# The first batch's stage rebuilt: weight words split in PSUM, V through DRAM, two taps in one GpSimd instruction, and new order tables

## The chip, the cores and the metric

The kernel runs on one core of one Trainium2 chip. The time is the device time of one execution in microseconds (us). Engines go by the profile's names: PE (TensorE matmuls), PEld (its weight loads), DVE (VectorE), ACT (ScalarE), POOL (GpSimd), SP (the engine that issues all of this kernel's DMAs).

## What is computed

A causal convolution over seven positions, with softmax weights per position and head, is followed by a low-rank mixing along the sequence and a two-layer network:

```python
w = softmax(weight_gen, axis=-1)                       # (8, 4224, 8 heads, 7 taps)
out[b, s, h, g] = sum_k w[b, s, h, k] * x_pad[b, s + k, h, g]    # 24 columns to a head
u = out + (out^T @ U @ V)^T                            # U: 4224 x 32, V: 32 x 4224
y = u + max(u @ w_ch1, 0) @ w_ch2                      # 192 -> 768 -> 192
```

Shapes are 8 batches of 4224 rows of 192 columns. `x` and `weight_gen` are float32. The four weights `U`, `V`, `w_ch1`, `w_ch2` come as float64, and the kernel reads them as pairs of 32-bit words.

## The kernel before

**Blocks and chunks.** Partition p holds the 33 rows p*33 to p*33+32 of a batch. Three of them on all partitions (384 rows) are a block `i`, 11 to a batch, 88 in all. The convolution of the same rows is chunk `c`. For a chunk each of the seven taps is one multiplication of 128x576 elements (`conv_mul`, tile `p`), and the products are added into the PSUM tile `acc`; the result is `y_c`.

**The stage of the first batch.** Before block 0 can start, all eleven chunks of batch 0 must be done, because the mixing needs their sum over the whole sequence (`z_first`, then `z_sum`, `z_split`, `z_copy`, which gives `zcat`). Chunk 11 of batch 1 is laid there too. In the same stage the weights are taken apart. A float64 is turned into a rounded fp32r part, and a remainder of what that leaves, by `f64_split`: in step 0 and 1 ACT converts the high and the low word, in 2 and 3 DVE shifts and sets the sign, in 4 ACT writes the rounded part, in 5 to 7 or 8 DVE makes the scale, the low word's value, the difference and the sum. There are twelve such sets (three of U, three of V, three of w1, three of w2); six have five DVE instructions and six have six, 66 in all. Their tiles (`..._t`, `..._s`, `..._lf`, `..._r`, `..._hi`, with the set's name ahead, `w_` for w2) lie in SBUF. V's parts are then put into `vcat` by 48 ACT copies of 32 partitions each (`v_copies`).

Taps of this stage are multiplied by POOL (weights from SBUF, tile `wr`) or by DVE (weights from a copy in PSUM, tile `wq`). The products are added by PE (a product with the identity `ident`, `conv_pe`), by DVE (`conv_add`), and the first one of a chunk by an ACT copy. The last addition of each chunk, which writes `y`, is DVE's.

**What sets the order.** Each engine carries out its instructions in the order in which the program lists them, and so does SP with its DMAs. The list is made by numbers: `at(time, work)` collects the pieces of work, and `issue()` emits them sorted by `time`. The tables `F_...` do so for the first stage, `GHI` to `ZM` for the blocks after it. A block has six time units. Its PE work is `mm1` (five matmuls for each of six tiles `h`, from `hi` and `lo`, the two parts of the transposed `u`) and `mm2` (into `ab`, from `gh` and `gl`); ACT makes `hi` and `gh`, DVE makes `lo`, `gl` and the output `o`, and ACT's `ab` seed fills `ab` before `mm2`. POOL goes on with the convolution about a batch ahead. The first block of a batch, and block 1 (`is_late`), take the transposed `u` from PSUM and not by way of DRAM.

```python
def u_lo(i, part):
    ...
    nc.vector.tensor_tensor(like(i, lo), u_from(i, part), like(i, hi[:n].bitcast(F32)), op=ALU.subtract)
```

The line number of nearly all instructions in the profile is 30, the helper that pins their order, so they are told apart by their tiles.

Of the kernel before, what the change touches and what calls it, by code (L numbers as in the profile page):

```python
# [44 lines left out]
def conv_moe_kernel(  # L45
# [23 lines left out]
    P = 128  # L69
# [35 lines left out]
    def fetch(n):  # L105

        if n >= len(PIECES):
# [77 lines left out]
    def f64_split(name, raw, n, hi, shaped, lo=None, rest=None, after=None):  # L185


        tiles = {}

        def tmp(what, dt=F32):  # L190
            if what not in tiles:
                tiles[what] = first.tile(
                    [P, CH], dt, tag=what, name=f"{name}_{what}",
                    bufs=3 if what in ("r", "hi", "lf") else 2,
                )[:, :n]
            return tiles[what]
# [12 lines left out]
        def ti():  # L209
            return tmp("t").bitcast(I32)  # L210
# [4 lines left out]
                tmp("t"), high.bitcast(F32), AF.Copy, scale=2.0**-112  # L215
            ),
            lambda: nc.scalar.copy(tmp("lf"), low.bitcast(U32)),
# [6 lines left out]
            lambda: nc.scalar.copy(top(), shaped(tmp("t"))),  # L224
# [4 lines left out]
                low_word(), shaped(tmp("lf")), 2.0**-52,  # L229
# [3 lines left out]
        if rest is not None:  # L233
            steps.append(
                lambda: nc.vector.tensor_tensor(
                    rem(), shaped(tmp("t")), top().bitcast(F32), op=ALU.subtract
                )
            )
        else:
            steps += [  # L240
                lambda: nc.vector.tensor_tensor(
                    shaped(tmp("r")), shaped(tmp("t")), top().bitcast(F32),
                    op=ALU.subtract,
                ),
                lambda: nc.vector.tensor_tensor(
                    rem(), shaped(tmp("r")), low_word(), op=ALU.add
                ),
            ]
# [69 lines left out]
    def prep_v():  # L318
# [3 lines left out]
        for p0 in range(0, PQ, step):  # L322
# [3 lines left out]
            for q in range(Q):  # L326
# [7 lines left out]
                after=lambda *parts: v_copies(p0, m, *parts),  # L334
            )

    def v_copies(p0, m, top, rem, low_word):
        def one(q, i):
            src = (top, rem, low_word, top)[i]().bitcast(F32)
            ps = q * R + p0  # L340
# [5 lines left out]
        return [lambda q=q, i=i: one(q, i) for q in range(P // R) for i in range(4)]  # L346
# [13 lines left out]
    def softmax(n_):  # L360
# [15 lines left out]
        nc.vector.tensor_scalar(sm, sm, 1e-9, None, op0=ALU.add)  # L376
# [27 lines left out]
    wqs = {}  # L404

    def conv_wq(c):
        n, jl = where[c]
        wq = ps_first.tile([P, 512], F32, tag="wq", name=f"wq_{c}", bufs=2)
        wqs[c] = wq[:, : T * H * K].rearrange("p (t h k) -> p t h k", t=T, h=H)
        nc.scalar.copy(wqs[c], ws[n][:, jl : jl + T])  # L410

    def conv_mul(c, k, mixed=False):
        n, jl = where[c]
        j = c % NB * T
        pool = pf if c < NB and k in (0, 2, 4) else pp
        pk = pool.tile([P, T, D], F32, tag="p", name=f"p_{c}_{k}")
        eng, w = (nc.vector, wqs[c]) if mixed else (nc.gpsimd, ws[n][:, jl : jl + T])
# [6 lines left out]
        prods[(c, k)] = pk  # L424

    def conv_done(c):
# [6 lines left out]
    def conv_first(c, pool):  # L433


        acc = pool.tile([P, 1024], F32, tag="acc", name=f"acc_{c}")
        accs[c] = halves(acc)
        if c > 1:
            nc.scalar.copy(accs[c], split3(prods.pop((c, 0))))
        else:  # L440
            conv_pe(c, 0)

    def conv_pe(c, k):

        pk = split3(prods.pop((c, k)))
        for i in range(2):
            nc.tensor.matmul(
                accs[c][:, i], ident, pk[:, i],
                start=(k == 0), stop=True, skip_group_check=True,
            )  # L450

# [172 lines left out]
    def d_tile(i, part, pool=None):  # L624
        d = (pool or ps_d).tile(
            [P, 512], F32, tag="wq" if pool else "d", name=f"d_{i}_{part}",
            bufs=2 if pool else 1,
# [193 lines left out]
    GHI = [0.683, 0.44, 0.78, 0.441, 0.818, 0.797]  # L821
    GLO = [1.427, 1.631, 1.807, 1.418, 1.153, 1.282]
    AB = [-0.507, -0.72, -0.687]
    OH = [2.136, 2.535, 1.934]
    OA = [2.941, 3.066, 2.841]
    UC = 5.253
    UT = -6.896
    UB = -5.473
    UH = [-1.541, -0.531]
    UL = [-1.009, -0.309]  # L830
    DS = [-2.383, -0.797]
    US = [-11.643, -8.974]
    UM = [-9.93, -8.655]
    UTK = [-9.566, -8.514]
    MUL = [-1.341, 0.905, -0.084, 1.787, 2.403, 2.46, 4.888]
    ADD = [1.149, 2.181, 3.355, 3.892, 4.643, 6.066]
    LA = 0.434
    SHORT = [15, 16, 17, 18, 19]
    SOFT = [-10.851, -8.336, -5.978, -4.698, -4.059, -2.592]
    DN = 1.833  # L840
    YH = 1.075
    YHL = 2.399
    YL = 4.355
    ZS = 5.19
    ZP = 6.235
    ZC = 6.666
    M1 = [-0.161, 0.323, -0.511, 0.043, -0.273, 0.135]
    M2 = [0.641, 0.346, 0.26, 0.394, -0.086, 0.837]
    DM = [-2.201, -0.724]
    ZM = 4.559  # L850
# [15 lines left out]
    F_FIRST = [6.54, 14.42, 17.88, 23.56, 30.37, 35.91, 37.83, 43.54, 50.85, 58.04, 61.28, 71.62]
# [144 lines left out]
```

## Time and profile before

| What | us |
|---|---|
| Median of 3 runs (lowest, highest) | 1141.16 (1139.52, 1141.96) |
| The profiled execution's own time | 1141.85 |
| Its span, from first to last instruction | 1139.8 |
| Busy in the span: PE, PEld | 1085.3, 1048.1 |
| Busy in the span: DVE, POOL, ACT | 995.1, 902.9, 831.7 |

The span is 2.05 us shorter than the time of the same execution. The share of busy time is an average over two unlike stages: PE is busy for 0.5 to 0.8 of the time in the first five of the page's 40 slices, and for 0.9 or more from then on, but for the last one. A row of a view by lines reads: engine, operation, tile written from tiles read, partitions x elements, count, then the busy time of the group, the mean of one in ns, and the idle time of the engine just before them.

### The profile page before, as it was taken

How to read it: one execution, taken by the hardware profiler on the slowest of the kernel's cores; microseconds unless marked ns; L12 is line 12 of the kernel's file. 1: busy time of each engine (PE TensorE's matmuls, PEld its weight loads, DVE VectorE, ACT ScalarE, POOL GpSimd, SP SyncE). 2: the span in 40 equal slices, each digit the busy share in tenths (PEclk: the TensorE clock that was granted, in tenths of full speed). 3: DMA queues.
4: the chain of work that ended last, by engine and by line, in shares of the span. 5: the costliest groups of instructions: out<-in, count | busy, mean ns of one | idle time of the engine just before them, and what ended most of it. 6: DMA issues, size and time to landing. Idle time of an engine off the chain costs nothing.

```text
span 1139.8 us, 20500 instructions
## 1 busy us (share of the span) xinstructions
PE 1085.3 (95%) x6619; PEld 1048.1 (92%) x6619; DVE 995.1 (87%) x1750; ACT 831.7 (73%) x1967; POOL 902.9 (79%) x719
## 2 busy tenths in 40 slices
PE   5786699999999999999999999999999999999998
PEld 3665599999999999999999999999999999999998
DVE  7998899999999999989999999999999989855553
ACT  5567477768777877778777877777777877776674
POOL 6784899999999999999999899999999899500000
PEclk8888799999999999999999999999999999999999
DMA  6223143434343443344334434344334332222321
GB/s 212 93 80 102 32 113 105 127 99 135 104 130 103 113 125 110 112 117 134 107 114 115 126 112 120 98 124 124 115 106 127 95 93 73 85 73 83 95 74 52
DMA packets 123308, 121.33 MB, mean 106 GB/s; under 512 B 78857, under 2 KB 97609, under 8 KB 123074
## 3 DMA queue, kind: packets, MB, share of 16 engines
q1 hardware_dynamic: 123202, 120.04, 36.4%
q8 instruction: 52, 0.85, 0.3%
q14 instruction: 54, 0.44, 0.1%
HBM read 68.38 MB, written 51.61 MB: 105 GB/s over the span
## 4 chain that ended last, share of the span: by engine, by line
PE 75%; DVE 13%; ACT 4%; issue 4%; POOL 2%; DMA 1%; SPq 0%; DVEq 0%; ACTq 0%; POOLq 0%
PE h L30 36%; PE ab L30 34%; PE zp L30 3%; DVE acc L30 2%; DVE lo L30 2%; ACT vcat L30 2%; PE u L30 2%; POOL p L30 2%; DVE sq L30 1%; DVE gl L30 1%; ACT gh L30 1%; DVE sm L30 1%; DVE p L30 1%; DVE o L30 1%; DVE y L30 1%
## 5 line engine op out<-in xcount | busy, mean ns | idle before, releaser
L30 POOL TENSOR_TENSOR p<-x,wr 128x576 f32<-128x576 f32 x585 | 735.7, 1289 | 44.5 <-DVE acc L30 26.9
L30 PE MATMUL ab<-w2c,gh 128*128 128x384 f32 x1584 | 511.6, 353 | 0.0
L30 ACT ACTIVATE gh<-h 128x384 fp32r<-128x384 f32 x528 | 260.4, 493 | 154.8 <-PE h L30 152.3
L30 PE MATMUL ab<-w2c,gl 128*128 128x192 f32 x1584 | 365.4, 256 | 0.0
L30 DVE SCALAR_TENSOR_TENSOR gl<-h,gh 128x384 fp32r<-128x384 f32 x528 | 286.8, 543 | 84.3 <-ACT gh L30 79.7
L30 DVE TENSOR_TENSOR acc<-acc,p 128x576 f32<-128x576 f32 x390 | 293.8, 753 | 18.2 <-ACT acc L30 14.1
L30 PEld LDWEIGHTS ab<-w2c,gh 128*128 128x128 f32 x1584 | 298.6, 189 | 0.2 <-ACT gh L30 0.2
L30 PEld LDWEIGHTS ab<-w2c,gl 128*128 128x128 f32 x1584 | 296.9, 189 | 0.0
L30 PE MATMUL h<-lo,w1s 128*128 128x384 f32 x528 | 181.9, 345 | 3.7 <-DVE lo L30 2.6
L30 PE MATMUL h<-hi,w1h 128*128 128x384 f32 x528 | 181.0, 343 | 1.0 <-DVE gl L30 0.9
L30 PE MATMUL h<-hi,w1s 128*128 128x384 f32 x528 | 179.9, 341 | 0.0
L30 PE MATMUL h<-hi,w1l 128*128 128x384 f32 x528 | 179.9, 341 | 0.0
L30 PE MATMUL h<-lo,w1h 128*128 128x384 f32 x528 | 179.4, 340 | 0.0
L30 ACT ACTIVATE ab<-u 128x384 f32<-128x384 f32 x264 | 130.4, 494 | 6.6 <-DVE o L30 6.0
L30 DVE TENSOR_TENSOR lo<-uT,hi 128x384 fp32r<-128x384 f32 (+1 forms) x158 | 126.8, 802 | 1.0 <-ACT hi L30 0.3
L30 ACT COPY o<-ab 128x192 f32<-128x192 f32 x264 | 85.2, 323 | 55.0 <-PE ab L30 55.0
L30 ACT CAST hi<-uT 64x384 fp32r<-64x384 f32 (+1 forms) x237 | 121.6, 513 | 1.9
L30 POOL TENSOR_TENSOR yhl<-y,yhl 128x576 fp32r<-128x576 f32 x77 | 111.0, 1441 | 11.3 <-ACT yhl L30 11.1
L30 PEld LDWEIGHTS h<-lo,w1s 128*128 128x128 f32 x528 | 99.5, 188 | 14.0 <-DVE lo L30 13.4
L30 PEld LDWEIGHTS h<-hi,w1h 128*128 128x128 f32 x528 | 100.9, 191 | 3.9 <-DVE gl L30 3.6
L30 DVE TENSOR_TENSOR o<-ab,o 128x192 f32<-128x192 f32 x264 | 91.5, 346 | 12.5 <-ACT o L30 7.7
L30 PEld LDWEIGHTS h<-hi,w1s 128*128 128x128 f32 x528 | 99.5, 188 | 0.4 <-ACT hi L30 0.4
(107 smaller groups left out, 1288.8 us busy)
## 6 DMA issues: line engine op xcount, KB each, us to landing
out_dram<-o SPq DMA_DIRECT2D x88, 288.0 KB, 2.8
turn<-sq SPq DMA_DIRECT2D x348, 72.0 KB, 1.9
x<-in_x_dram SPq DMA_DIRECT2D x77, 288.0 KB, 3.6
uT<-turn SPq DMA_DIRECT2D x87, 192.0 KB, 2.4
uT<-turn SPq DMA_DIRECT2D x87, 96.0 KB, 2.5
wr<-in_weight_gen_dram SPq DMA_DIRECT2D x15, 336.0 KB, 4.1
x<-in_x_dram SPq DMA_DIRECT2D x7, 504.0 KB, 5.5
wr<-in_weight_gen_dram SPq DMA_DIRECT2D x9, 252.0 KB, 3.9
```

The costliest lines, as they stand in the source:

```text
L30: return self.tc.keep_in_program_order(call(*args, **kwargs))
```

## The change

Five things are changed.

1. `f64_split` keeps the words in PSUM: `t` in the bank of pool `ps_d`, the low word and the first difference in one bank `px` (tiles `pt_..._t` and `pt_..._x`). The low word's product, the scale `s` and the rounded part stay in SBUF.
2. V's parts are stored to DRAM (nine stores), read back into a tile `vq` of all 128 partitions (sixteen loads, one `vq` buffer), and put into `vcat` by four ACT copies.
3. POOL multiplies two taps in one instruction of 128x1152 elements (`conv_mul2`): of the 84 taps of the stage 46 go in 23 such pairs and 8 alone on POOL, 30 on DVE (before: 53 alone on POOL, 31 on DVE). The weights for DVE's taps now share one PSUM bank of three slots.
4. The additions: before, PE has 52 of them and DVE 22, eleven of which wrote `y` in batch 0 and one in chunk 11. After, PE has 59, DVE 16, and ACT copies eleven finished sums to `y`. The +1e-9 of the softmax goes from DVE to ACT, in the whole kernel.
5. The first stage's order is a written list, `FIRST`, instead of times, and 29 of the 30 tables for the blocks have new numbers.

```diff
@@ f64_split
+        def bank(what):
+            if what not in tiles:
+                pool, tag = (ps_d, "d") if what == "t" else (ps_first, "px")
+                tiles[what] = pool.tile([P, 512], F32, tag=tag, name=f"pt_{name}_{what}")[:, :n]
+            return tiles[what]
...
         def ti():
-            return tmp("t").bitcast(I32)
+            return bank("t").bitcast(I32)
...
-            lambda: nc.scalar.copy(tmp("lf"), low.bitcast(U32)),
+            lambda: nc.scalar.copy(bank("x"), low.bitcast(U32)),
...
-                    shaped(tmp("r")), shaped(tmp("t")), top().bitcast(F32),
+                    shaped(bank("x")), shaped(bank("t")), top().bitcast(F32),
                     op=ALU.subtract,
@@ V
-            nc.scalar.copy(
-                vcat[i * R : (i + 1) * R, :, ps : ps + m],
-                src[q * R : (q + 1) * R].rearrange("r (p j) -> r j p", j=NJ),
-            )
+            nc.sync.dma_start(
+                vts[i][:, p0 * NJ : p0 * NJ + n], parts[i]().bitcast(F32)
+            )
...
+    def v_load(q):
+        PQ = P // (P // R)
+        vqs[q] = first.tile([P, PQ * NJ], F32, tag="vq", name=f"vq_{q}", bufs=1)
+        for i, k in enumerate((0, 1, 2, 0)):
+            nc.sync.dma_start(
+                vqs[q][i * R : (i + 1) * R], vts[k][q * R : (q + 1) * R]
+            )
+
+    def v_place(q):
+        PQ = P // (P // R)
+        nc.scalar.copy(
+            vcat[:, :, q * PQ : (q + 1) * PQ],
+            vqs.pop(q).rearrange("r (p j) -> r j p", j=NJ),
+        )
@@ softmax
-        nc.vector.tensor_scalar(sm, sm, 1e-9, None, op0=ALU.add)
+        nc.scalar.activation(sm, sm, AF.Copy, bias=1e-9)
+        yield
@@ convolution
+    def conv_mul2(c, k):
+
+        n, jl = where[c]
+        j = c % NB * T
+        pk = pf.tile([P, 2, T, D], F32, tag="p2", name=f"p_{c}_{k}{k + 1}")
+        x0 = xt[:, j + k : j + k + T, :]
+        w0 = ws[n][:, jl : jl + T, :, k]
+        nc.gpsimd.tensor_tensor(
+            pk.rearrange("p k t (h g) -> p k (t h) g", h=H),
+            bass.AP(
+                tensor=x0.tensor, offset=x0.offset,
+                ap=[x0.ap[0], [D, 2], [G, T * H], [1, G]],
+            ),
+            bass.AP(
+                tensor=w0.tensor, offset=w0.offset,
+                ap=[w0.ap[0], [1, 2], [K, T * H], [0, G]],
+            ),
+            op=ALU.mult,
+        )
...
+    def conv_copy(c):
+        y = yp.tile([P, T, D], F32, tag="y", name=f"y_{c}")
+        nc.scalar.copy(split3(y), accs.pop(c))
+        ys[c] = y
@@ tables of the blocks (two of 29)
-    UH = [-1.541, -0.531]
+    UH = [-1.831, -0.529]
-    AB = [-0.507, -0.72, -0.687]
+    AB = [-0.793, -0.666, -0.577]
...
@@ the first stage's order
+    FIRST = """
+        R W1 S0 x0 S0 S0 U0 S1 S0 S1 S0 S0 S1 S0 Q0 S1 U1 M0.0v S1 M0.1d S1 P0.0 F0.0t x1
...
+        d1 C9.3 Y11.6
```

In `FIRST` a letter names the work and the numbers what it is for: P is a step of a split set, M a multiplication (by v DVE, p POOL, d POOL for two taps), F and A additions, Y a finished chunk.

How the change moves instructions is read off the two programs, at three places. Names are as in the profile with their numbers: `w22` and `w24` are two sets of w2, `p_11_6` is tap 6 of chunk 11, `p_11_45` the pair of its taps 4 and 5.

DVE at the end of the first stage, before:

```order
L30 TENSOR_SCALAR w22_s_795<-w22_t_682 128x384
L30 TENSOR_TENSOR w24_r_797<-w24_t_752,w2c_108 128x384
L30 SCALAR_TENSOR_TENSOR w22_lf_693<-w22_lf_693,w22_s_795 128x384
L30 TENSOR_TENSOR w22_r_807<-w22_t_682,w2c_108 128x384
L30 SCALAR_TENSOR_TENSOR w24_lf_755<-w24_lf_755,w24_s_793 128x384
L30 TENSOR_TENSOR w2c_108<-w22_r_807,w22_lf_693 128x2x192
L30 TENSOR_TENSOR w2c_108<-w24_r_797,w24_lf_755 128x2x192
L30 TENSOR_TENSOR zcat_0_826<-zr_0_820,zcat_0_826 32x192
L30 TENSOR_TENSOR acc_11_818<-acc_11_818,p_11_3_813 128x2x288
L30 TENSOR_TENSOR acc_11_818<-acc_11_818,p_11_1_824 128x2x288
L30 TENSOR_TENSOR p_11_6_838<-x_90,wq_11_801 128x576
L30 TENSOR_TENSOR lo1_0_109<-d_0_1_809,hi1_0_835 64x384
```

The same place after:

```order
L30 TENSOR_TENSOR acc_11_732<-acc_11_732,p_11_12_721 128x2x288
L30 TENSOR_SCALAR w24_s_756<-pt_w24_t_728 128x384
L30 TENSOR_TENSOR acc_11_732<-acc_11_732,p_11_12_721 128x2x288
L30 SCALAR_TENSOR_TENSOR w24_lf_765<-pt_w24_x_739,w24_s_756 128x384
L30 TENSOR_TENSOR pt_w24_x_739<-pt_w24_t_728,w2c_108 128x384
L30 TENSOR_TENSOR acc_11_732<-acc_11_732,p_11_45_749 128x2x288 x2
L30 TENSOR_TENSOR w2c_108<-pt_w24_x_739,w24_lf_765 128x2x192
L30 TENSOR_TENSOR y_11_789<-acc_11_732,p_11_6_767 128x576
L30 TENSOR_TENSOR zcat_0_795<-zr_0_793,zcat_0_795 32x192
L30 TENSOR_TENSOR lo0_0_801<-d_0_0_780,hi0_0_799 128x384
L30 TENSOR_TENSOR lo1_0_109<-d_0_1_784,hi1_0_804 64x384
```

Where two sets of w2 stood back to back, with all operands in SBUF, one set now stands between the additions of chunk 11, each of its instructions with an operand in PSUM; chunk 11 ends ahead of `zcat` and not after `lo`.

POOL at the start of the first stage, before:

```order
L30 TENSOR_TENSOR wr_0_92<-wr_0_92,mx_0_137 128x168
L30 TENSOR_TENSOR wr_0_92<-wr_0_92,sm_0_138 128x168
L30 TENSOR_TENSOR p_0_2_146<-x_90,wr_0_92 128x576
L30 TENSOR_TENSOR p_0_5_156<-x_90,wr_0_92 128x576
L30 TENSOR_TENSOR wr_1_130<-wr_1_130,mx_1_163 128x504
L30 TENSOR_TENSOR p_0_3_179<-x_90,wr_0_92 128x576
L30 TENSOR_TENSOR p_0_1_186<-x_90,wr_0_92 128x576
```

The same place after:

```order
L30 TENSOR_TENSOR wr_0_92<-wr_0_92,mx_0_126 128x168
L30 TENSOR_TENSOR wr_1_124<-wr_1_124,mx_1_136 128x504
L30 TENSOR_TENSOR wr_0_92<-wr_0_92,sm_0_127 128x168
L30 TENSOR_TENSOR p_0_12_159<-x_90,wr_0_92 128x1152
L30 TENSOR_TENSOR wr_1_124<-wr_1_124,sm_1_137 128x504
L30 TENSOR_TENSOR p_0_56_183<-x_90,wr_0_92 128x1152
```

The softmax of the second piece of weights (`wr_1`) moves ahead of the first taps, and the taps go in pairs.

ACT in a block after the first stage (blocks 35 and 36), before:

```order
L30 ACTIVATE gh_35_4_7050<-h_35_4_7030 128x384
L30 CAST hi1_36_7072<-uT1_36_6936 64x384 x2
L30 ACTIVATE ab_35_0_7075<-u_35_6642 128x384
L30 ACTIVATE gh_35_5_7081<-h_35_5_7063 128x384
L30 COPY o_34_6938<-ab_34_2_7014 128x192
```

The same place after:

```order
L30 ACTIVATE gh_35_4_7004<-h_35_4_6985 128x384
L30 ACTIVATE ab_35_0_7010<-u_35_6598 128x384
L30 CAST hi1_36_7020<-uT1_36_6869 64x384 x2
L30 ACTIVATE gh_35_5_7030<-h_35_5_7012 128x384
L30 COPY o_34_6891<-ab_34_2_6976 128x192
```

The seed of `ab` now stands ahead of the two copies that make `hi1` for the next block. PE's own order in the blocks is the same but for `zr`, one matmul in a batch (fp32, as two passes), which stands one `mm1` tile later.

More of the change, by code (lines that the diff above doesn't have):

```diff
@@ L333, in prep_v, with v_stores, one @@
                 f"v{p0}", raw, n, None, flat, rest=True,
-                after=lambda *parts: v_copies(p0, m, *parts),
+                after=lambda *parts: v_stores(p0, n, *parts),
             )
[L337 to L340, printed above, removed]
-            nc.scalar.copy(
-                vcat[i * R : (i + 1) * R, :, ps : ps + m],
-                src[q * R : (q + 1) * R].rearrange("r (p j) -> r j p", j=NJ),
-            )
-        return [lambda q=q, i=i: one(q, i) for q in range(P // R) for i in range(4)]
+    vts = []
+    def v_stores(p0, n, *parts):
+        while len(vts) < NU:
+            vts.append(
+                dram.tile(
+                    [P, P // (P // R) * NJ], F32, tag=f"vt{len(vts)}",
+                    name=f"vt{len(vts)}", bufs=1,
+                )
+            )
+        def one(i):
+            nc.sync.dma_start(
+                vts[i][:, p0 * NJ : p0 * NJ + n], parts[i]().bitcast(F32)
+            )
+        return [lambda i=i: one(i) for i in range(NU)]
+    vqs = {}
+    def v_load(q):
[11 more added lines that the diff above has]
+        )
     works = {}
@@ L424, in conv_mul @@
         prods[(c, k)] = pk
+    def conv_mul2(c, k):
[15 more added lines that the diff above has]
+            op=ALU.mult,
+        )
+        for i in range(2):
+            prods[(c, k + i)] = pk[:, i]
     def conv_done(c):
@@ L448, in conv_pe, with conv_vector, conv_last @@
                 accs[c][:, i], ident, pk[:, i],
-                start=(k == 0), stop=True, skip_group_check=True,
+                start=begin, stop=True, skip_group_check=True,
             )
+    def conv_vector(c, k):
+        acc = accs[c]
+        nc.vector.tensor_tensor(acc, acc, split3(prods.pop((c, k))), op=ALU.add)
+    def conv_copy(c):
+        y = yp.tile([P, T, D], F32, tag="y", name=f"y_{c}")
+        nc.scalar.copy(split3(y), accs.pop(c))
+        ys[c] = y
+    def conv_last(c, k):
+        y = yp.tile([P, T, D], F32, tag="y", name=f"y_{c}")
+        nc.vector.tensor_tensor(
+            split3(y), accs.pop(c), split3(prods.pop((c, k))), op=ALU.add
+        )
+        ys[c] = y
     accs = {}
@@ new lines, in conv_moe_kernel @@
+    DS = [-2.436, -0.869]
+    US = [-11.65, -8.874]
+    UM = [-9.793, -8.798]
+    UTK = [-9.258, -8.463]
+    MUL = [-1.341, 1.206, -0.084, 1.462, 2.534, 2.46, 4.808]
+    ADD = [1.149, 2.101, 3.355, 3.866, 4.615, 6.279]
+    LA = 0.659
+    SHORT = [15, 16, 17, 18, 19]
+    SOFT = [-9.854, -7.411, -5.03, -4.293, -6.756, -3.712, -3.227]
+    DN = 1.925
+    YH = 1.011
+    YHL = 0.839
+    YL = 2.929
+    ZS = 5.206
+    ZP = 6.344
+    ZC = 6.726
+    M1 = [0.517, 0.011, -0.164, 0.107, -0.273, 0.378]
@@ L887, in conv_moe_kernel @@
-        for n in range(5):
-            for time in F_SOFT[n]:
-                at(time, soften, n)
-        for c in range(NB + 1):
-            at(F_WQ[c], conv_wq, c)
-            for k in range(K):
-                at(F_MUL[c][k], conv_mul, c, k, F_BY[c][0][k] == "v")
-            at(F_DONE[c], conv_done, c)
-            at(F_FIRST[c], conv_first, c, ps_a if c % 2 else ps_first)
-            for k in range(1, K):
-                at(F_ADD[c][k - 1], conv_pe if F_BY[c][1][k - 1] == "t" else conv_add, c, k)
-            if c < NB:
-                at(F_Z[c], z_first, c)
@@ L900, in conv_moe_kernel @@
-        at(F_TURN[0], u_turn, 1)
-        at(F_TURN[1], u_back, 1)
-        for time, work in zip(F_END, (
-            (z_sum, 0), (z_split, 0), (z_copy, 0), (d_turn, 0, 0), (d_mix, 0, 0),
-            (u_hi, 0, 0), (u_lo, 0, 0), (d_turn, 0, 1), (d_mix, 0, 1), (u_hi, 0, 1),
-            (u_lo, 0, 1),
-        )):
-            at(time, *work)
-        issue()
+        segs = ((0, 9), (9, 18), (18, 30), (30, 39))
+        for code in FIRST.split():
+            kind, by = code[0], code[-1]
+            n = [int(i) for i in code[1:].rstrip("pdvta").split(".") if i]
+            if kind == "U":
+                prep_load(n[0], kinds[F_KIND[n[0]]])
+            elif kind == "P":
+                prep_step(*n)
+            elif kind == "C":
+                copy_one(*n)
+            elif kind == "W":
+                fetch(*n)
+            elif kind == "x":
+                x_load(0, *segs[n[0]])
+            elif kind == "S":
+                soften(*n)
+            elif kind == "Q":
+                conv_wq(*n)
+            elif kind == "M":
+                conv_mul2(*n) if by == "d" else conv_mul(*n, by == "v")
+            elif kind == "D":
+                conv_done(*n)
+            elif kind == "F":
+                conv_first(*n, by)
+            elif kind == "A":
+                conv_pe(*n) if by == "t" else conv_vector(*n)
+            elif kind == "Y":
+                conv_last(*n) if len(n) == 2 else conv_copy(*n)
+            elif kind == "L":
+                v_load(*n)
+            elif kind == "V":
+                v_place(*n)
+            elif kind == "Z":
+                z_first(*n)
+            elif kind == "R":
+                make_rsum()
+            elif kind == "T":
+                u_turn(*n)
+            elif kind == "B":
+                u_back(*n)
+            elif kind == "d":
+                d_turn(0, *n)
@@ L909, in conv_moe_kernel @@
+        z_sum(0)
+        z_split(0)
+        z_copy(0)
+        for part in range(2):
+            d_mix(0, part)
+            u_hi(0, part)
+            u_lo(0, part)
     gp = ctx.enter_context(tc.tile_pool(name="gp", bufs=2 * NM))
```

140 lines of the change are left out of this document (62 added, 78 removed).

## The prediction

> **What bounds the kernel now.** I read the busy time by stretches first, cut where the first stage ends.
>
> ```profile
> core 0: us, PE busy (x) PEld busy (x) DVE busy (x) ACT busy (x) POOL busy (x), PEclk, DMA share, GB/s
> 0.00:8.00 8.00, 0.00 (x0) 0.00 (x0) 2.14 (x8) 2.13 (x4) 2.80 (x10) 1.00 0.75 192
> 8.00:121.00 113.00, 78.47 (x282) 59.12 (x282) 103.52 (x132) 70.71 (x115) 80.03 (x61) 0.84 0.33 109
> 121.00:125.00 4.00, 1.94 (x5) 1.36 (x6) 3.83 (x7) 1.90 (x4) 2.36 (x2) 0.50 0.00 0
> 125.00:248.00 123.00, 119.03 (x717) 113.40 (x716) 116.28 (x201) 89.92 (x216) 121.31 (x97) 0.98 0.37 103
> 248.00:1004.00 756.00, 754.00 (x4778) 743.37 (x4777) 699.82 (x1262) 579.07 (x1409) 696.44 (x551) 1.00 0.39 112
> 1004.00:1139.80 135.80, 131.85 (x843) 130.83 (x841) 69.52 (x143) 87.99 (x222) 0.00 (x0) 1.00 0.25 74
> ```
>
> There are two kernels in one. From 125 us on PE has work in 1004.9 of 1014.8 us: nothing there can gain more than some 10 us without fewer matmuls. Up to 125 us DVE is the full engine: 103.5 of 113 us, against 80 for POOL, 78 for PE and 71 for ACT. Next the groups of that stage, and single instructions from the timeline.
>
> ```profile
> L30 DVE SCALAR_TENSOR_TENSOR w_lf<-w_lf,w_s 128x384 f32<-128x384 f32 x3 | 4.4, 1463 | 0.0
> L30 DVE TENSOR_TENSOR w_r<-w_t,w2c 128x384 f32<-128x384 f32 x3 | 3.7, 1218 | 0.0
> L30 DVE TENSOR_SCALAR w_s<-w_t 128x384 int32<-128x384 int32 x3 | 2.8, 971 | 0.0
> L30 DVE TENSOR_TENSOR w2c<-w_r,w_lf 128x384 fp32r<-128x384 f32 x3 | 2.6, 885 | 0.0
> L30 DVE SCALAR_TENSOR_TENSOR w_t<-w,w_t 128x384 int32<-128x384 int32 x3 | 1.6, 546 | 0.0
> L30 DVE TENSOR_SCALAR w_t<-w_t 128x384 int32<-128x384 int32 x3 | 1.5, 525 | 0.0
> L30 DVE TENSOR_TENSOR lo<-d,hi 128x384 fp32r<-128x384 f32 x1 | 0.5, 540 | 0.0
> L30 DVE TENSOR_TENSOR p<-x,wq 128x576 f32<-128x576 f32 x31 | 21.9, 739 | 3.0 <-DMA x<-in_x_dram 3.0
> L30 DVE TENSOR_TENSOR y<-acc,p 128x576 f32<-128x576 f32 x11 | 8.2, 741 | 0.0
> L30 DVE TENSOR_TENSOR rsum<-ident 96x128 f32<-96x128 f32 x1 | 1.3, 1284 | 0.0
> L30 POOL TENSOR_TENSOR p<-x,wr 128x576 f32<-128x576 f32 x55 | 72.8, 1350 | 19.8 <-PE acc L30 8.3 <-DVE y L30 3.9 <-ACT acc L30 2.8
> ```
>
> ```profile
> 99.31 1.21 POOL L30 TENSOR_TENSOR p<-x,wr 128x576 f32<-128x576 f32 x1 [0.96 <-PE acc L30]
> ...
> 104.15 0.55 DVE L30 TENSOR_TENSOR w_r<-w_t,w2c 128x384 f32<-128x384 f32 x1
> ...
> 106.56 0.58 DVE L30 TENSOR_SCALAR w_t<-w_t 128x384 int32<-128x384 int32 x2
> ...
> 109.89 1.36 POOL L30 TENSOR_TENSOR wr<-wr,sm 128x672 f32<-128x672 f32 x1 [6.08 <-DVE sm L30]
> ...
> 111.34 8.39 POOL L30 TENSOR_TENSOR p<-x,wr 128x576 f32<-128x576 f32 x6
> ...
> 114.16 1.55 DVE L30 SCALAR_TENSOR_TENSOR w_lf<-w_lf,w_s 128x384 f32<-128x384 f32 x1
> ...
> 124.84 0.52 PE L30 MATMUL h<-hi,w1h 128*128 128x384 f32 x1
> ```
>
> The reader is to see one thing. The same kind of DVE instruction takes 0.55 us at 104 us, in a pause of POOL, and 1.55 us at 114 us, while POOL multiplies; POOL's taps take 1.40 each there (8.39 for six) and 1.21 alone. DVE instructions with an operand in PSUM (`lo<-d,hi` 540 ns, `p<-x,wq` 739, `y<-acc,p` 741) show no such spread. So most of DVE's load is waiting for POOL inside all-SBUF instructions.
>
> **DVE's sum.** To the end of chunk 11 DVE has 2.14+103.52+3.83 = 109.5 us, and four additions of chunk 11 follow after 125 us (4 x 0.74 = 3.0): 112.5.
> - Words in PSUM: the six groups of w2 average 935 ns. With a PSUM operand I take 540, the row of `lo<-d,hi` with the same 384 elements. 66 x 0.395 = 26.1 saved. Bounds: nothing saved, if the word operand left in SBUF still collides; 66 x (0.935-0.29) = 42 if PSUM kept the 0.29 of the two instructions at 106.56. I take 540 because that row has the operands' places that the new ones have.
> - Additions 22 to 16: 6 x 0.74 = 4.4. One multiplication less: 0.7. The softmax's five small additions are not counted. `rsum` at the start, without POOL beside it, 0.54 and not 1.28, twice: 1.4.
> - Sum: 112.5 - 32.6 = 79.9.
>
> Here is the rule that speaks against the edit. The row at 106.56 is a shift at 0.29 us with both operands in SBUF. The Trainium skill (VectorE: DVE Perf Modes, "Why PSUM operands drop a tier") says that the fast mode needs both SBUF read ports, so a PSUM operand holds fp32 to one element a cycle. By it, 24 shifts and masks lose 0.25 us each, 6 us, against a sum with 0.29 for them; the sum above has them at 540 already, and no run here shows a shift in PSUM yet.
>
> **When the stage ends.** DVE's first tap waits for x:
>
> ```profile
> 7.81 1.42 DVE L30 TENSOR_TENSOR p<-x,wq 128x576 f32<-128x576 f32 x2 [2.96 <-DMA x<-in_x_dram]
> ```
>
> The load of `wr_1` (258 KB) now goes ahead of x; at the 192 GB/s of that stretch it costs 1.3 us: 9.1. Before that DVE does about 4.5 us (the 2.14 of before, `rsum`, the reductions of `wr_1`). That leaves 75.4, so the stage ends at 9.1 + 75.4 + idle time. Idle time was 113 - 103.5 = 9.5; I take 12, since POOL and PE are now nearly as full as DVE and buffers are as few. First matmul of `h`: about 96.5 us, where it was 124.8. Saved: 28.3.
>
> **The other engines, whether they allow that.**
> - POOL: 85.2 us to 125, 5.4 of it for four taps of chunk 12. 53 taps at 1.35 (71.6) become 8 at 1.21 and 23 pairs. A pair lies between 2.17 (1.21 and 576 more elements at the slope of the rows below, 0.279 us for 168) and 2.70 (two of today's). I take 2.2, as nothing else blocks POOL then: 79.8 - 71.6 + 60.3 = 68.5. About 5 of it lies ahead of x: 9.1 + 63.5 = 73, below DVE's 84.5.
>
> ```profile
> L30 POOL TENSOR_TENSOR wr<-wr,mx 128x672 f32<-128x672 f32 x2 | 2.7, 1360 | 0.5 <-DVE mx L30 0.5
> L30 POOL TENSOR_TENSOR wr<-wr,mx 128x504 f32<-128x504 f32 x2 | 2.2, 1081 | 5.9 <-issue 5.8
> L30 PE MATMUL acc<-p,ident 128*128 128x288 f32 x208 | 66.3, 486 | 34.1 <-DVE p L30 15.7 <-DVE w_t L30 8.1 <-ACT acc L30 4.2
> L30 ACT CAST vcat<-v_hi 32x363 fp32r<-32x363 f32 x16 | 13.6, 850 | 0.3
> L30 ACT CAST vcat<-v_hi 32x330 fp32r<-32x330 f32 x8 | 6.3, 785 | 0.1
> L30 ACT COPY acc<-p 128x576 f32<-128x576 f32 x10 | 6.4, 639 | 2.0 <-DVE p L30 1.3 <-POOL p L30 0.6
> L30 ACT COPY wq<-wr 128x168 f32<-128x168 f32 x12 | 3.4, 297 | 7.3 <-POOL wr L30 4.1 <-DVE p L30 3.1
> ```
>
> - PE: 208 matmuls took 66.3 us at a mean granted clock of 0.84, 0.319 each. Seven more taps make 236: 9 us more. 78.5 + 1.9 + 9 = 89, from 9 to 98, were it never better fed; at full clock 0.84 of that, 84. PE is next in line, not first.
> - ACT: the 48 copies of V cost 32 x 0.850 + 16 x 0.785 = 39.8. The four new ones have 1056 elements: 1.0 by the slope of the two COPY rows, 2.2 by that of the two vcat rows; I take 1.7, together 7. Eleven `y` copies at 0.64 add 7.0, the five small additions less than 0.3 each (168 elements take 0.297), so 1. 74.7 - 39.8 + 15 = 50: free.
> - SP: 25 more transfers, in the queue that also brings x and the raw words, behind stores that wait for DVE. A store landed in 1.9 us and a load in 2.4 in the rows below; through one `vq` buffer the four rounds take 4 x (2.4 + 1.7 + 0.5) = 18 us, started with about 24 us of DVE work left by the new list. Covered; without that cover `vcat` would hold back `d_mix` by what is missing.
>
> ```profile
> turn<-sq SPq DMA_DIRECT2D x348, 72.0 KB, 1.9
> uT<-turn SPq DMA_DIRECT2D x87, 192.0 KB, 2.4
> ```
>
> What is late next at the stage's end: `zcat`, `hi`, `lo`, which DVE now reaches after chunk 11 and which nothing shortens.
>
> **The blocks.** PE's order is unchanged but for `zr`; its lost time is in waits on DVE's `lo`.
>
> ```profile
> PEld h L30 <- DVE lo L30: 13.4, 31, 1.1
> ```
>
> ```profile
> 470.80 1.04 ACT L30 CAST hi<-uT 64x384 fp32r<-64x384 f32 x2
> ...
> 472.18 0.49 ACT L30 ACTIVATE ab<-u 128x384 f32<-128x384 f32 x1 [0.35 <-DVE o L30]
> ```
>
> ```profile
> 473.87 0.65 DVE L30 TENSOR_TENSOR lo<-uT,hi 64x384 fp32r<-64x384 f32 x1
> ```
>
> In this block `hi1` was ready at 471.84 and used at 473.87, so the seed put ahead of it (0.49) fits. The transposes that lie ahead of `lo` stay ahead. I take 1.5 us saved: chunk 11 no longer competes with block 0. Bounds: 10 saved (all of PE's gaps), 4 lost (the seed's 0.49 in a tenth of the blocks, an estimate).
>
> **Sum.** 1141.85 (profiled execution) - 28.3 - 1.5 = 1112.0. The median of the runs is 0.7 lower: 1111.
>
> **Rivals.**
> - POOL becomes the bound. At 2.70 a pair POOL has 80 us, 75 of them after 9.1: 84, level with DVE, and I reckon that two full engines that wait for each other's buffers idle for 20, not 12: first `h` at 104.5, **1119**. For it: 19.8 us of POOL's waits are already on PE, DVE and ACT. The Trainium skill (GPSIMD Engine Reference, "Elementwise — side-by-side cycle accounting") gives two-input work 2.6 cycles an element at 1.2 GHz; an estimate from it is 2.5 us for a pair, between my ends, with POOL below DVE still.
> - The new tables also remove the waits on `lo` and early gaps, 8 more: **1104**. For it: the gap budget of 10; against: nothing ahead of `lo` on DVE moves.
> - Slower: the seed ahead of `hi1`. The seed waits for DVE's `o`; if `hi1` then comes late in each of the 79 blocks (88 less the nine of `is_late`, which take `hi` from PSUM), 79 x 0.49 = 39 lost, 1141.85 - 30 + 39 = **1151**. It decides from 0.38 us a block. Against: the 2 us of room above.
> - PSUM does not help: DVE keeps 935 ns, and only additions, `rsum` and chunk 11's place count: **1134**.
>
> **How the numbers follow.** Main case 0.55 (1105 to 1117), POOL 0.20, tables 0.17, PSUM 0.04, slower 0.04. The range 1099 to 1124 holds the first three with their idle time. 0.2% (2.3 us) is about what can be told from no change: faster 0.95, same 0.02, slower 0.03.
>
> **What would show it.** First `h` matmul near 96.5 us; DVE's `pt_..._t` groups at 540 ns with little spread; POOL's single taps at 1.2 and pairs at 2.2; four vcat copies under 2.2; `zcat` of the last batch 883.6 us behind that of the first, as now (120.6 and 1004.2):
>
> ```profile
> L30 DVE TENSOR_TENSOR zcat<-zr,zcat x8: 362/363/365, 120.6 to 1004.2; 32x192 fp32r<-32x192 f32 x8
> ```
>
> I am wrong if DVE idles over 20 us in the stage, or if a block grows by 0.3.

## The result, and the profile after

The changed kernel takes **1100.41 us** (median of 4 runs, 1099.95 to 1101.72) beside 1140.59 for the kernel before on the same chip (4 runs): ratio 0.9649, 95% interval 0.9632 to 0.9666, 40.2 us less. Forecast were 1111 us and a range of 1099 to 1124.

The busy time by stretches of the changed kernel, cut where its first stage ends (columns as in the same view of before):

```profile
core 0: us, PE busy (x) PEld busy (x) DVE busy (x) ACT busy (x) POOL busy (x), PEclk, DMA share, GB/s
0.00:8.00 8.00, 0.00 (x0) 0.00 (x0) 3.61 (x11) 3.14 (x7) 3.72 (x11) 1.00 0.76 211
8.00:85.00 77.00, 73.36 (x312) 57.78 (x312) 70.40 (x125) 44.97 (x85) 74.60 (x44) 1.00 0.68 208
85.00:90.00 5.00, 3.52 (x11) 3.55 (x12) 1.38 (x3) 2.08 (x5) 0.35 (x1) 0.56 0.00 0
```

PE, DVE and POOL are now all over nine tenths full in the stage, and PE's granted clock there went from 0.84 to 1.00. The timeline gives the stage's two ends, and the row of `zcat` the length of the blocks (from its first time, 83.5, to its last, 962.9):

```profile
7.91 0.75 DVE L30 TENSOR_TENSOR p<-x,wq 128x576 f32<-128x576 f32 x1 [0.41 <-ACT sm L30]
...
87.25 0.52 PE L30 MATMUL h<-hi,w1h 128*128 128x384 f32 x1
```

```profile
L30 DVE TENSOR_TENSOR zcat<-zr,zcat x8: 362/364/365, 83.5 to 962.9; 32x192 fp32r<-32x192 f32 x8
```

The first `h` comes 37.6 us earlier (124.84 before). From there to the end of the span it is 1011.6 us, 3.4 less than before; from the first `zcat` to the last 879.4, 4.2 less. So over nine tenths of the gain lies in the first stage. Groups of that stage, those that the prediction priced:

```profile
L30 POOL TENSOR_TENSOR p<-x,wr 128x1152 f32<-128x1152 f32 x23 | 50.7, 2219 | 1.7 <-DMA x<-in_x_dram 1.4 <-PE acc L30 0.3
L30 POOL TENSOR_TENSOR p<-x,wr 128x576 f32<-128x576 f32 x18 | 21.2, 1198 | 1.5 <-PE acc L30 1.5
L30 DVE TENSOR_SCALAR pt_w_t<-pt_w_t 128x384 int32<-128x384 int32 x3 | 1.7, 563 | 0.2 <-ACT pt_w_t L30 0.2
L30 DVE SCALAR_TENSOR_TENSOR w_lf<-pt_w_x,w_s 128x384 f32<-128x384 f32 x3 | 1.7, 551 | 0.0
L30 DVE TENSOR_SCALAR w_s<-pt_w_t 128x384 int32<-128x384 int32 x3 | 1.6, 549 | 0.0
L30 PE MATMUL acc<-p,ident 128*128 128x288 f32 x236 | 61.4, 420 | 8.9 <-DVE p L30 8.8
L30 ACT CAST vcat<-vq 128x1056 fp32r<-128x1056 f32 x4 | 8.5, 2134 | 2.8 <-DMA vq<-vt 2.8
L30 ACT COPY y<-acc 128x576 f32<-128x576 f32 x11 | 7.0, 638 | 8.1 <-PE acc L30 8.1
```

`w_lf`, 1463 ns before, takes 551 with its low word in PSUM. Over all 66 word instructions the sum of the records falls from 64.2 to 35.5 us, the mean from 973 to 538 ns, the longest from 1.55 to 0.57 us.

### The profile page after: what moved, and what is told of

Read it like the earlier page. It is cut to its first block, busy times and chain, and to the rows that moved or that the text cites. A ratio compares the mean times of both kernels' runs of the same rounds, so it can differ in the third digit from the quotient of the medians.

```text
span 1098.8 us, 20367 instructions
## 1 busy us (share of the span) xinstructions
PE 1077.1 (98%) x6647; PEld 1047.1 (95%) x6647; DVE 945.2 (86%) x1718; ACT 816.4 (74%) x1958; POOL 890.8 (81%) x697
## 4 chain that ended last, share of the span: by engine, by line
PE 85%; DVE 5%; POOL 3%; DMA 2%; ACT 2%; issue 2%; SPq 1%; DVEq 0%; ACTq 0%
PE h L30 39%; PE ab L30 38%; PE zp L30 3%; POOL p L30 2%; PE u L30 2%; PE acc L30 2%; DMA x<-in_x_dram 1%; DVE acc L30 1%; DMA vq<-vt 1%; SPq L30 1%; DVE lo L30 1%; DVE p L30 1%; POOL yhl L30 1%; DVE gl L30 0%; ACT vcat L30 0%
## 5 line engine op out<-in xcount | busy, mean ns | idle before, releaser
L30 POOL TENSOR_TENSOR p<-x,wr 128x576 f32<-128x576 f32 (+1 forms) x563 | 723.7, 1317 | 17.5 <-DVE acc L30 14.3
L30 DVE TENSOR_TENSOR acc<-acc,p 128x576 f32<-128x576 f32 x395 | 296.8, 751 | 18.8 <-ACT acc L30 13.5
L30 PE MATMUL h<-hi,w1h 128*128 128x384 f32 x528 | 178.8, 339 | 0.8 <-DVE gl L30 0.8
L30 DVE TENSOR_TENSOR lo<-uT,hi 128x384 fp32r<-128x384 f32 (+1 forms) x158 | 120.5, 763 | 3.0 <-ACT hi L30 2.4
L30 POOL TENSOR_TENSOR yhl<-y,yhl 128x576 fp32r<-128x576 f32 x77 | 110.5, 1435 | 13.2 <-ACT yhl L30 13.2
L30 PEld LDWEIGHTS h<-hi,w1l 128*128 128x128 f32 x528 | 99.6, 189 | 0.0
```

Of the source, the lines that this page charges most:

```text
L30: return self.tc.keep_in_program_order(call(*args, **kwargs))
```

## The experiments

Each is the changed kernel with one or two things altered. First `h` is the first matmul of `h` in the profiled execution, the third column the time from the first `zcat` to the last, also there. Each ratio is to the kernel before on the same chip, whose medians were 1139.69 to 1141.57 us, so medians of two rows can differ by 1 to 2 us through the chip alone.

| Kernel | First `h`, us | `zcat`, us | Median, us | Ratio to before, 95% |
|---|---|---|---|---|
| Before | 124.84 | 883.6 | 1140.59 | |
| Changed | 87.25 | 879.4 | 1100.41 | 0.9632 to 0.9666 |
| Words in SBUF | 124.40 | 878.9 | 1136.74 | 0.9952 to 0.9977 |
| Words in SBUF, single taps | 113.21 | 880.4 | 1127.16 | 0.9859 to 0.9886 |
| Single taps | 87.74 | 878.9 | 1100.70 | 0.9643 to 0.9672 |
| V by 48 copies | 122.11 | 878.5 | 1135.99 | 0.9955 to 0.9981 |
| V by 48 copies, spread | 105.29 | 878.4 | 1119.74 | 0.9795 to 0.9821 |
| `y` copied by DVE | 91.97 | 878.9 | 1104.58 | 0.9678 to 0.9705 |
| Old tables | 88.30 | 896.3 | 1114.15 | 0.9759 to 0.9800 |
| Old tables, addition on DVE | 87.02 | 881.6 | 1103.94 | 0.9656 to 0.9688 |
| New tables, addition on DVE | 87.25 | 885.9 | 1107.20 | 0.9684 to 0.9711 |
| Cast first | 86.71 | 878.9 | 1099.94 | 0.9643 to 0.9673 |
| Cast first, PE kept busy | 86.83 | 877.9 | 1099.96 | 0.9643 to 0.9678 |

**Words back in SBUF.**

```diff
-                pool, tag = (ps_d, "d") if what == "t" else (ps_first, "px")
-                tiles[what] = pool.tile([P, 512], F32, tag=tag, name=f"pt_{name}_{what}")[:, :n]
+                tiles[what] = first.tile(
+                    [P, CH], F32, tag=f"pt{what}", name=f"pt_{name}_{what}", bufs=1,
+                )[:, :n]
```

> Theory (VectorE's word instructions with all operands in SBUF lose time beside GpSimd; a PSUM operand takes that loss away): back in SBUF, with the new order, pairs and V by way of DRAM kept, the 66 word instructions average 0.8 to 1.0 us instead of 0.55, which is 17 to 28 us more for VectorE; first matmul of h at 105 to 114 us (87.25 in the changed kernel), time 1118 to 1127 us; GpSimd's pairs slower too, 2.4 to 2.8 us. Rival (the order, the V copies and the pairs brought the gain): words slow again but idle time takes it up, first matmul of h before 93 us, time under 1107 us.

The first `h` came at 124.40, where it was before the change: nearly the whole gain of the stage is gone, and more than the theory allowed; POOL's pairs took 2.404 us, as it had said. The words average 1.161 us, longer than before the change (0.973), and twenty of the 66 are over 1.6 us, the longest 2.58. The timeline of this kernel, DVE's rows and then POOL's, shows what such an instruction does:

```profile
62.65 0.32 DVE L30 TENSOR_SCALAR pt_v_t<-pt_v_t 128x330 int32<-128x330 int32 x1
...
64.08 2.37 DVE L30 TENSOR_SCALAR v_s<-pt_v_t 128x330 int32<-128x330 int32 x1
```

```profile
59.15 2.52 POOL L30 TENSOR_TENSOR p<-x,wr 128x1152 f32<-128x1152 f32 x1
64.05 2.22 POOL L30 TENSOR_TENSOR p<-x,wr 128x1152 f32<-128x1152 f32 x1 [2.38 <-PE acc L30]
```

A shift and a mask of the same shape: the one at 62.65, in POOL's pause, takes 0.32 us; the one at 64.08 begins 0.03 us behind a pair and ends 0.18 us behind the pair's end (66.45 and 66.27). It waits for the whole pair. If the wait is always the rest of the POOL instruction that is under way, the change's pairs about double the longest one; the next experiment puts that to the test.

The Trainium skill (SBUF — State Buffer, "Who interferes with whom") says that DVE's second pair of SBUF ports is also POOL's, and that when a DVE instruction of the kind that uses both pairs meets a POOL instruction, whoever issues first has the shared pair for its whole instruction while the other is blocked. The two rows agree: the pair began first, and the mask ended behind it.

**Words in SBUF and single taps.** The same, and each pair as two instructions of 576 elements into the same buffers (the diff of the next experiment).

> Words in SBUF as in the run before this one that had them there, and GpSimd's pairs as two single taps. There 66 word instructions averaged 1.16 us, up to 2.58; before the change 0.97, up to 1.55. Theory: a VectorE instruction with all operands in SBUF that begins beside a GpSimd instruction waits until that one ends, so its longest is GpSimd's instruction and 0.3 us more. With taps of 1.2 us the longest word is 1.5 to 1.6 us and the mean 0.90 to 1.0, 11 to 17 us less for VectorE: first matmul of h at 107 to 115 us, time 1119 to 1128 us. Rival (GpSimd's load counts, not the length of one instruction): mean 1.1 to 1.2 as with the pairs, first matmul of h at 121 to 126 us, time 1133 to 1138 us.

First `h` 113.21, words 0.971 us in the mean and 1.56 at most: what they were before the change. POOL lost too: its taps took 1382 ns in this kernel, 1201 with the words in PSUM. The theory holds, and the runs give the price of the words. In PSUM they are worth 113.21 - 87.74 = 25.5 us beside single taps, and 124.40 - 87.25 = 37.2 beside pairs.

**Single taps, words in PSUM.**

```diff
-        nc.gpsimd.tensor_tensor(
-            pk.rearrange("p k t (h g) -> p k (t h) g", h=H),
...
+        for i in range(2):
+            nc.gpsimd.tensor_tensor(
+                pk[:, i].rearrange("p t (h g) -> p t h g", h=H),
+                xt[:, j + k + i : j + k + i + T, :].rearrange("p t (h g) -> p t h g", h=H),
+                ws[n][:, jl : jl + T, :, k + i].unsqueeze(3).to_broadcast([P, T, H, G]),
+                op=ALU.mult,
+            )
```

> All as in the changed kernel, but each GpSimd pair is two instructions of 576 elements into the same buffers. If GpSimd sets the pace now (74.6 of 77 us busy), all of 23 x (2 x 1.20 - 2.22) = 4.1 us is lost: first matmul of h at 91 to 92, time 1104 to 1105 us. If VectorE or TensorE sets it, or the earlier first half pays it back: first matmul of h within 1.5 us of 87.25, time 1099 to 1102 us.

First `h` 0.5 us later, the time as in the changed kernel. The pairs gain nothing that can be measured here; beside words in SBUF they cost 124.40 - 113.21 = 11.2 us. POOL is the fullest engine of the stage, but not the one that sets its end: up to 88 us it does 14 single taps in the changed kernel, and the stage needs eight of them; the rest belong to later chunks.

**V by the 48 ACT copies.**

```diff
-            nc.sync.dma_start(
-                vts[i][:, p0 * NJ : p0 * NJ + n], parts[i]().bitcast(F32)
-            )
+            src = parts[i]().bitcast(F32)
+            for q in range(P // R):
+                for r in (i, 3)[: 2 - (i > 0)]:
+                    nc.scalar.copy(
+                        vcat[r * R : (r + 1) * R, :, q * R + p0 : q * R + p0 + m],
+                        src[q * R : (q + 1) * R].rearrange("r (p j) -> r j p", j=NJ),
+                    )
```

> All as in the changed kernel, but V is laid out by the 48 ScalarE copies of before and not by way of DRAM. ScalarE gets 48 copies of 0.83 us (39.8 in all) for the four casts of 2.13 (8.5): 45 + 31 = 76 us busy of the 77 between x and the first matmul of h. Theory (V by way of DRAM is needed now, since ScalarE would be as full as the other engines): first matmul of h 4 to 15 us later, at 91 to 102, time 1104 to 1116 us. Rival (ScalarE lies off the path, the V part gave nothing): first matmul of h within 2 us of 87.25, time within 2 us of 1100.4.

First `h` 122.11: far more is lost than either theory had. ACT is not full (76 of 112 us), but its copies come in one piece, since each place that a store had in the list now holds four or eight of them. Its timeline shows such a piece, and the waits of that stage (us in total, times, longest) show who stands behind them:

```profile
66.17 6.35 ACT L30 CAST vcat<-v_hi 32x330 fp32r<-32x330 f32 x8
72.52 6.57 ACT L30 CAST vcat<-v_lf 32x330 fp32r<-32x330 f32 x8
79.12 0.51 ACT L30 ACTIVATE pt_w1a_t<-w1a 128x384 f32<-128x384 f32 x1
```

```profile
PE acc L30 <- ACT wq L30: 12.6, 1, 12.6
...
DVE pt_w1a_t L30 <- ACT pt_w1a_t L30: 11.3, 2, 10.8
DVE sm L30 <- ACT wr L30: 10.4, 2, 10.0
```

This happens twice. Around 27 to 42 us DVE waits 10.0 us for ACT's `wr` and POOL 13.2 us for DVE's `sm` behind it; around 69 to 89 us DVE waits 10.8 us for the `pt_w1a_t` above, and PE, further down the same chain, 12.6 us for `wq`. Each time a small ACT step that the others need is queued behind the copies. The expectation had set ACT's total beside the stage's length and left out the order on ACT.

**V by 48 copies, spread.** One copy after every third other step of the list.

> V laid out by the 48 ScalarE copies as in the run that had them, where they came in bursts of up to 16 (0.83 us each) and the time was 1136.0 us, first matmul of h at 122.1; here one copy after every third other step of the list, so at most a few follow each other (a fourth pair of buffers holds V's words longer). ScalarE's busy time stays 31 us above the changed kernel's 45. If the bursts held up the queue (copies of wq, of sums and exponentials behind them): first matmul of h at 89 to 101 us, time 1102 to 1114 us. If ScalarE's load itself sets the pace: first matmul of h still behind 110 us, time over 1123 us.

First `h` 105.29, between the two: the bursts were 17 us of the loss, and 18 us stay.

```profile
8.00:105.00 97.00, 80.47 (x313) 62.10 (x314) 72.59 (x126) 78.34 (x131) 75.38 (x44) 0.93 0.39 126
```

ACT has 78 of 97 us, no engine is full, and what holds the 18 us that stay is open. Whether a list made for the copies would lose less wasn't tried. What is shown: in this list V by way of DRAM is worth 18 us beside evenly spread copies and 35 beside copies in bursts, and ACT, which I had called free, is free because of it.

**`y` copied by DVE.**

```diff
-        nc.scalar.copy(split3(y), accs.pop(c))
+        nc.vector.tensor_copy(split3(y), accs.pop(c))
```

> All as in the changed kernel, but the eleven copies of y in the first stage stand on VectorE (about 0.74 us each, 8.2 in all) and not on ScalarE. Splitting GpSimd's pairs, some 3.5 us more of GpSimd's time, moved the first h by 0.5 us alone. If VectorE (70.4 us busy of 77) sets the pace, most of the 8.2 shows: first matmul of h at 92 to 96 us (87.25), time 1105 to 1109 us. If its idle time takes the copies up: first matmul of h by 89.5, time under 1103 us.

The copies took 8.2 us on DVE (750 ns each); the first `h` came 4.7 us later and the time was 4.2 us longer. That lies at the low edge of the first case and just short of it in time: DVE passes on rather more than half of what it is given, POOL about an eighth (0.5 of 23 x (2 x 1.20 - 2.22) = 4.1). So of the two DVE is the nearer to a bound, but not alone. PE has more work than DVE in the stage (73.4 against 70.4 of 77 us), and what it would pass on wasn't tried.

**The old tables.** The changed first stage, and the blocks' numbers of before (the softmax's addition of 1e-9, which is now a step of its own on ACT, at the place of the reduction ahead of it).

> All as in the changed kernel, but the places of the steady blocks' steps come from the tables of before; the first stage's list stays new. First matmul of h as in the changed kernel, 87 to 88 us. If the new tables gave the 3.5 us that the time after the first h fell by: time 1103 to 1105 us, last zcat 882 to 884 us after the first (879.4 with the new tables, 883.6 before). If those 3.5 us came from a first stage that leaves less work behind it: time 1099.5 to 1101.5 us.

Neither: from the first `zcat` to the last the blocks became 16.9 us longer than with the new tables, and 12.7 longer than in the kernel before, whose tables these are. The profiled execution took 1118.25 us, 4.1 more than the median, so by the medians the blocks lose about 13 us and not 17. In the groups from 400 to 900 us of the two kernels, `lo` has changed (changed kernel first):

```profile
L30 DVE TENSOR_TENSOR lo<-uT,hi 128x384 fp32r<-128x384 f32 x39 | 37.2, 954 | 0.0
```

```profile
L30 DVE TENSOR_TENSOR lo<-uT,hi 128x384 fp32r<-128x384 f32 x39 | 50.5, 1294 | 0.0
```

Before it was 990 ns. The timeline with the old tables, DVE and then POOL:

```profile
449.66 1.61 DVE L30 TENSOR_TENSOR lo<-uT,hi 128x384 fp32r<-128x384 f32 x1
```

```profile
449.64 2.69 POOL L30 TENSOR_TENSOR p<-x,wr 128x576 f32<-128x576 f32 x2
```

It is the wait of the words again: `lo` has both operands in SBUF, begins 0.02 us behind a tap and waits for its end. Of the 39 `lo` of that stretch 15 take 1.47 us or more; in the changed kernel none takes over 1.25. The one other edit to the blocks' instructions is the addition moved to ACT; the next two kernels put it back.

**The addition back on DVE, with old and with new tables.**

```diff
-        nc.scalar.activation(sm, sm, AF.Copy, bias=1e-9)
+        if n_ < 5:
+            nc.scalar.activation(sm, sm, AF.Copy, bias=1e-9)
         yield
+        if n_ >= 5:
+            nc.vector.tensor_scalar(sm, sm, 1e-9, None, op0=ALU.add)
```

> The changed kernel's first stage, the old tables, and in the blocks the softmax addition of 1e-9 back on VectorE as before the change. Old tables with that addition on ScalarE took 1114.2 us and their lo<-uT of 128x384 averaged 1.29 us between 400 and 900 us (0.95 in the changed kernel, 0.99 before). Theory: the addition's 0.2 to 0.34 us on VectorE shifted VectorE against GpSimd's taps, and without it lo begins just behind a tap's start and waits for its end; with it back lo is 0.97 to 1.01, last zcat 883 to 885 us after the first, time 1103 to 1106 us. Rival (something else in the change slows the blocks under the old tables): lo stays at 1.25 or more, time 1112 to 1116 us.

> The changed kernel with its new tables, but in the blocks the softmax addition of 1e-9 back on VectorE. If tables and the addition's place only fit together (each set holds lo out of the taps for one place of the addition): lo of 128x384 over 1.05 us, time 1103 to 1114 us. If the new tables are good with both: lo 0.93 to 0.98, time 1099.5 to 1101.5 us.

Old tables with the addition on DVE: 1103.94 us, `zcat` 881.6 and `lo` 936 ns, a little less than the theory's 883 and 970. The timeline there:

```profile
432.21 0.55 DVE L30 TENSOR_TENSOR lo<-uT,hi 128x384 fp32r<-128x384 f32 x1
```

```profile
431.09 3.89 POOL L30 TENSOR_TENSOR p<-x,wr 128x576 f32<-128x576 f32 x3
```

Here `lo` begins at about the border of two taps (431.09 + 1.17 = 432.26, an estimate with the 1.17 us from tap to tap of five taps in a row, 5.85 us, in the changed kernel) and takes 0.55. New tables with the addition on DVE: 1107.20 us, inside the range of the first case; `lo` is 1001 ns, between the two cases. So of the four combinations the two that were made for each other take 1100.4 and 1103.9, the mixed ones 1107.2 and 1114.2. By the third column of the table both edits together gain 2.2 us over neither; the new tables alone lose 4.3, and the addition's move alone loses 14.7. By the medians these are 3.5, 3.3 and 10.2: the directions are clear, the sizes are not. `lo` explains the direction, not the size: in the mixed kernel with the new tables it is 47 ns longer than in the changed kernel, 3.7 us over 79 blocks, of 6.5; with the old tables it is 340 ns longer, 27 us over 79 blocks, and the blocks lose only 13 to 17.

**Cast first, and PE kept busy.** Two tries for a faster version. In the changed kernel's timelines DVE, and behind it PE, wait at the stage's end for a cast of ACT that stands behind the last V copy:

```profile
79.75 0.57 DVE L30 TENSOR_TENSOR pt_w_x<-pt_w_t,w2c 128x384 f32<-128x384 f32 x1 [1.50 <-ACT w2c L30]
```

```profile
82.29 0.52 PE L30 MATMUL d<-ident,y 128*64 128x128 f32 x3 [1.35 <-DVE w2c L30]
```

```diff
-        V3 Z7 P11.5 Z8 Y10 P11.4 A11.2v
+        P11.4 V3 Z7 P11.5 Z8 Y10 A11.2v
```

> One step of the list moved: the last weight part's cast of w2c on ScalarE goes ahead of the last V copy (2.12 us), behind which VectorE's pt_w_x waited 1.50 us for it in the changed kernel and TensorE's d another 1.35 us for VectorE's w2c. Theory: that chain ends the stage, so the first matmul of h comes 0.8 to 1.5 us earlier, at 85.7 to 86.5, time 1098.9 to 1099.7 us. Rival: the V copy is now late itself, or zp's matmuls up to 80.6 us hold the sum anyway: first matmul of h 87.0 to 87.6, time as in the changed kernel.

Both waits went, but the first `h` came only 0.5 us earlier: DVE now does the same instructions without a pause up to 82.4, and `zp` ends 0.7 us later on PE, held by the later copy of `y`. In the time nothing can be measured.

```diff
+        keep_warm(5)
         z_sum(0)
         z_split(0)
+        keep_warm(5)
         z_copy(0)
...
+        keep_warm(7)
```

> As the run with the cast moved, and 17 matmuls of 128x128 whose result nothing reads stand in TensorE's waits at the end of the first stage (5 ahead of zr, 5 behind it, 7 behind the second d). In the changed kernel the granted clock fell to 0.50 from 86 to 92 us, and the first 20 matmuls of block 0 came every 0.32 us, where they come every 0.17 us at full clock. Theory: with TensorE busy through the waits the clock stays near 1.00 and block 0 ends 2 to 3 us sooner: time 1096 to 1098 us. Rival: block 0 is then held by ScalarE's and VectorE's gh and gl, or the added matmuls delay the stage's last steps by as much: within 0.7 us of the run with the cast moved.

The stretches with and without the added matmuls (first the run with the cast moved alone):

```profile
85.00:90.00 5.00, 4.04 (x13) 3.75 (x14) 1.11 (x2) 2.09 (x5) 1.07 (x2) 0.66 0.00 0
```

```profile
85.00:90.00 5.00, 4.29 (x27) 3.81 (x26) 1.86 (x4) 3.16 (x7) 1.62 (x2) 1.00 0.01 3
```

The granted clock stays at 1.00 and block 1 begins at 95.73 in place of 96.35 us: 0.6 us, not 2 to 3, and the medians are equal. Block 0 is then held by other engines: PE waits there for DVE's `gl` and ACT's `hi`. There was also less to gain than the expectation had reckoned, since it took the slow clock from the changed kernel, where it lasts from 86 to 92 us; with the cast moved the granted clock is back at 1.00 from 90 us. Neither kernel is measurably faster than the changed one.

## Why the prediction was right, and where it was off

The predicted 1111 is 10.6 us above the result. In the profiled executions 9.2 us of it lie in the first stage (96.5 forecast, 87.25 found) and 2 in the blocks. Of the 9.2, DVE's start is 1.2, its work 3.9 and its idle time 4.2 (from 7.91 to 87.25 it was busy for 71.5 us and idle for 7.8).

The result lies inside the range, but below the 1105 to 1117 of the main case, nearest to the 1104 of the rival with the tables. That rival is not what happened, since the blocks gave 3.4 us and not 9.5: the main case's mechanism held, with three of its terms too large on the same side.

- **Words, 26.1 us.** Mechanism and price hold: 538 ns against 540. The count of what they cost before was a little low: I averaged w2's six groups (935 ns), and all 66 averaged 973, so the records fell by 28.7. Between the two runs with single taps they fall by 28.6 and first `h` by 25.5, so that 25.5 lies so close to 26.1 is partly luck. That most of DVE's load was waiting for POOL was too much said: 28.7 of its 109.5 us went. That the pairs would have made words in SBUF dearer I missed; the edits are not a sum.
- **DVE's other terms.** The softmax's five additions (1.3 us), which I left out, and `rsum` (1.9, not 1.4) are most of the rest. DVE was busy for 74 us up to 85 us, and the sum 79.9 was about 6 too high.
- **Start at 9.1.** Wrong: DVE's first tap came at 7.91 and not 1.3 later. Before it came at 7.81. POOL's first pair, which waited for x, began at 7.94, so the load of `wr_1` ahead of x cost some 0.1 us.
- **Idle time, 12 us.** The term that was off most, by a little. From 8 to 85 us DVE idled 6.6, and some 1.3 more up to the first `h`. As a share of the stretch that is what it was (6.6 of 77, 9.5 of 113), though POOL and PE were fuller. I had reckoned that full engines wait more for each other; with this list they didn't.
- **POOL.** 2.2 a pair, 1.2 a tap: found 2.219 and 1.198. The rival with POOL as the bound fell, and splitting the pairs showed it: 0.5 us.
- **PE and ACT.** PE next in line: 73.4 of 77 us, at clock 1.00. ACT 48 us to 85, forecast 50; `vcat` copies 2.13, at the upper of my bounds and not 1.7. To call ACT "free" was right for the changed kernel and hid that the V edit is a condition for the gain.
- **V by DRAM.** The four rounds were covered: ACT waited 2.8 us for them, 1.1 at the longest.
- **Blocks, 1.5 us.** Found 3.4, inside the bounds, but not by what I gave as the reason, chunk 11: with the changed first stage, the old tables and the addition on DVE, the median less first `h` is 1016.9 us, where it was 1015.8 before. That "nothing ahead of `lo` on DVE moves" overlooked the addition that left DVE. The change holds a loss of some 10 us or more there, and the tables that take it back.
- **The slower rival.** The seed does wait for DVE's `o`, as the rows of the waits show (100 to 1090 us of the changed kernel), but a late `hi1` behind it would show in PE's waits on `lo`, and these fell to 10.1 from 13.4.

```profile
ACT ab L30 <- DVE o L30: 46.8, 78, 1.3
...
PEld h L30 <- DVE lo L30: 10.1, 30, 1.2
```

- **The rule that spoke against the edit.** By the Trainium skill (VectorE: DVE Perf Modes, "Why PSUM operands drop a tier") a shift in PSUM would lose the fast mode. It does: 563 ns for `pt_w_t`, against 0.29 us in SBUF in a pause of POOL. The loss was in the sum, and the avoided waits are worth far more.

What stays open: the new list of the first stage and the move of additions from DVE to PE were not run apart from the rest. The losses of the single experiments, 25.5 for the words and 18 for V among them, add up to more than the stage's 37.6, so they are not shares of the gain.

## What to carry to other kernels

Look for all-SBUF DVE instructions whose durations spread from one price up to that price plus a POOL instruction: here they waited for POOL, and one input in PSUM made them steady. Making POOL's instructions longer raised that wait, so move the words first and pair the taps after. And a step moved from one in-order engine to another shifts everything behind it against POOL: judge it by the long instructions that it shifts, not by its own 0.3 us, and price a queue by what stands behind a burst, not by its total.

## What had not been expected of the hardware

- A DVE instruction with its operands in SBUF waited for the whole POOL instruction under way: 2.37 us for a mask that begins beside a pair of 2.22, where a shift of the same shape took 0.32 in a pause. POOL pays as well, 1.38 us a tap against 1.20.
- Whether that wait is met repeats from batch to batch: in the changed kernel the `lo` at 420.10, 545.77, 671.46 and 797.14 us, one batch apart, take 0.85 us each. The same list of DVE instructions but for one of 0.2 to 0.34 us gave `lo` 0.94 or 1.29 us in the mean.
- Seventeen matmuls that nothing reads held PE's granted clock at 1.00, and 0.6 us up to block 1 was all that it was worth.
